# Three row blocks of the first Wq issued from ScalarE's queue behind a GpSimd memset

## The chip, the cores and the metric

The kernel runs on one core of one Trainium2 chip. The metric is the device time of one launch in microseconds (us), from the first instruction to the last. The kernel before takes 1230.46 us (median of three runs, 1230.24 to 1230.65).

## What is computed

The reference is a stack of two equal layers on 2048 tokens of 1024 features in bf16. Each layer is a sliding, dilated attention block (32 heads, window of 8 tokens at distance 2) followed by a dense block:

```
x = A_x
repeat twice:
    x = x + attention(layernorm(x), wqkv, wo)
    x = x + (gelu(layernorm(x) @ w1 + b1) @ w2 + b2)
```

Only the very first step matters here: the layer norm of the first tokens of x, and their product with Wq, which is the first third of the columns of wqkv (1024 rows, 3072 columns).

## The kernel before

The tokens go through the kernel in groups of 512, so there are four groups in each of the two layers, and a group is made of four x tiles of 128 tokens. TensorE (PE) does the matmuls one group and one stage after the other: query, key and value projections, attention output, first and second dense matmul. The other engines work beside it: VectorE (DVE) does the layer norms and the attention products, ScalarE (ACT) moves results out of PSUM and applies functions, GpSimd (POOL) does small operations and some transfers, and SyncE (SP) issues the loads.

**How order is set.** The kernel is written in a tile framework that puts in the semaphore waits. The wrapper `InOrder` around an engine adds order-only edges: while its `on` flag is set, each instruction recorded on this engine comes behind the one recorded before it; otherwise the framework's scheduler may move an instruction. PE's instructions are always chained in the written order. The framework gives every transfer issued by SP or ACT one of eight completion semaphores in turn (called lanes here, 0 to 7), and makes a transfer wait for the earlier transfer on its lane to land before it is issued. The first eight transfers wait for nothing.

**The start.** Before any stage, the kernel issues loads from SP: x tiles 0 and 1, then the first Wq in four pieces with x tiles 2 and 3 between them (`load_wq_piece`, lines 134 to 142). A piece is two row blocks of 128 rows by 1024 columns, 512 KB. `k` numbers the eight row blocks, and a matmul of contraction block `k` needs row block `k` only. A dummy Sqrt (line 151) makes ACT load its table early. `warm_up(14)` gives PE 14 matmuls on zeros while it waits for x.

Then `ln_first` (line 224) normalises the first two x tiles by hand: DVE takes the statistics of tile 0 and tile 1 (`bn_stats`, `bn_aggr`), ACT takes the square roots (`std`, line 238), DVE takes reciprocals and writes the normalised tiles `xn`, PE transposes them, and ACT and DVE copy the transposes out of PSUM into `xnT`. Inside `ln_first` both DVE and ACT are in written order. `build_constants` follows it and fills a mask with GpSimd memsets.

After that `gen_qkv(0)` begins: PE goes over the contraction blocks in four quarters of two `k` each, and within a quarter over seven of eight output chunks, on the 256 tokens of the first two tiles. So the first quarter needs row blocks 0 and 1 of Wq, the second 2 and 3, and so on. Tiles 2 and 3 are transposed on PE in the third and the fourth quarter.

## Time and profile before

| | PE | DVE | ACT | POOL |
|---|---|---|---|---|
| busy us in the span of 1228.4 us | 1221.6 | 861.5 | 315.6 | 120.9 |
| share of the span | 99% | 70% | 26% | 10% |

PE is busy all the time but for the first microseconds. "Busy" on PE also counts the 14 warm-up matmuls, which do no useful work. Over the whole span the loads move 226.64 MB, at 185 GB/s in the mean, with the first two slices of the span (some 61 us) at 302 and 290 GB/s. For this change one has to look at the first 15 us alone: what PE waits for there, and when each transfer is issued and lands. In the listings below SPq is SP's queue of transfers; a "landing" is the time from a transfer's issue to its completion.

### The profile page before, as it was taken

How to read it: one execution, taken by the hardware profiler on the slowest of the kernel's cores; microseconds unless marked ns; L12 is line 12 of the kernel's file. 1: busy time of each engine (PE TensorE's matmuls, PEld its weight loads, DVE VectorE, ACT ScalarE, POOL GpSimd, SP SyncE). 2: the span in 40 equal slices, each digit the busy share in tenths (PEclk: the TensorE clock that was granted, in tenths of full speed). 3: DMA queues.
4: the chain of work that ended last, by engine and by line, in shares of the span. 5: the costliest groups of instructions: out<-in, count | busy, mean ns of one | idle time of the engine just before them, and what ended most of it. 6: DMA issues, size and time to landing. Idle time of an engine off the chain costs nothing.

```text
span 1228.4 us, 13955 instructions
## 1 busy us (share of the span) xinstructions
PE 1221.6 (99%) x5720; PEld 632.7 (52%) x5770; DVE 861.5 (70%) x912; ACT 315.6 (26%) x497; POOL 120.9 (10%) x219
## 2 busy tenths in 40 slices
PE   9999999999999999999999999999999999999998
PEld 7666544456444564446544465444654444444444
DVE  7999896998898999375993759937599797011001
ACT  5343253014310233202431024410244001300310
POOL 2330025010101101100001000000000002000000
PEclk9999999999999999999999999999999999999999
DMA  9965674766638645856557565576664558446441
GB/s 302 290 206 164 176 233 151 202 178 199 219 128 245 188 150 166 239 170 175 161 158 230 172 171 181 157 216 201 171 200 147 186 194 209 149 159 194 156 135 52
DMA packets 223647, 226.64 MB, mean 185 GB/s; under 512 B 71824, under 2 KB 190752, under 8 KB 221536
## 3 DMA queue, kind: packets, MB, share of 16 engines
q1 hardware_dynamic: 214704, 208.69, 56.3%
q0 software_dynamic: 8880, 17.07, 4.2%
q8 instruction: 45, 0.74, 0.2%
q14 instruction: 18, 0.15, 0.0%
HBM read 189.01 MB, written 4.19 MB: 157 GB/s over the span
## 4 chain that ended last, share of the span: by engine, by line
PE 99%; DVE 0%; issue 0%; DMA 0%
PE acc L117 99%; DMA x<-in_A_x_dram 0%; DVE stats L92 0%; PE acc L211 0%; DVE xn L92 0%; DVE x L92 0%; DVE mv L92 0%; DVE rstd L92 0%
## 5 line engine op out<-in xcount | busy, mean ns | idle before, releaser
L117 PE MATMUL acc<-xnT,wt 128*128 128x512 bf16 (+1 forms) x3392 | 720.3, 375 | 0.1
L117 PEld LDWEIGHTS <-wt 128*128 128x128 bf16 x3392 | 400.8, 120 | 317.4
L117 PE MATMUL acc<-wt,hT 128*128 128x512 bf16 (+1 forms) x1780 | 386.0, 376 | 2.1
L117 PEld LDWEIGHTS <-hT 128*128 128x128 bf16 x1820 | 178.1, 98 | 209.0
L92 DVE TENSOR_TENSOR big<-big 128x1024 bf16<-128x1024 bf16 (+2 forms) x184 | 244.8, 1359 | 2.2
L92 ACT ACTIVATE hT<-acc,b1T 128x512 bf16<-128x512 f32 x224 | 152.1, 687 | 325.9 <-PE acc L117 325.8
L92 DVE TENSOR_TENSOR big<-qT,kT 128x4096 bf16<-128x4096 bf16 x64 | 143.8, 2283 | 36.3 <-ACT kT L92 35.9
L92 DVE TENSOR_TENSOR big<-abc,vT 128x4096 bf16<-128x4096 bf16 x64 | 144.6, 2284 | 11.0 <-DMA abc<-a 7.1
L92 DVE TENSOR_TENSOR tmp<-acc,b2bc 128x512 f32<-128x512 f32 x56 | 38.6, 689 | 159.8 <-PE acc L117 156.7
L92 ACT CAST qT<-acc 128x512 bf16<-128x512 f32 (+1 forms) x72 | 38.0, 543 | 276.8 <-PE acc L117 274.6
L117 PE MATMUL acc<-wt,oT 128*128 128x512 bf16 x440 | 97.6, 379 | 0.4
L92 DVE BATCH_NORM_STATS2 stats<-x 128x6 f32<-128x512 bf16 x116 | 77.4, 681 | 6.0 <-DMA x<-in_A_x_dram 5.0
L117 PEld LDWEIGHTS <-oT 128*128 128x128 bf16 x448 | 43.8, 98 | 53.0 <-issue 0.3
L92 DVE TENSOR_TENSOR x<-acc,big 128x512 bf16<-128x512 f32 (+1 forms) x9 | 5.7, 632 | 90.0 <-PE acc L117 90.0
L92 POOL TENSOR_TENSOR rstd<-mv,eps_t 128x1 f32<-128x1 f32 x54 | 16.7, 308 | 524.2 <-DVE mv L92 524.2
L92 ACT CAST vT<-acc 128x512 bf16<-128x512 f32 x64 | 37.4, 585 | 101.9 <-PE acc L117 101.9
L92 ACT CAST kT<-acc 128x512 bf16<-128x512 f32 x64 | 37.3, 584 | 64.5 <-PE acc L117 64.5
L92 DVE TENSOR_TENSOR x<-acc,x 128x512 bf16<-128x512 f32 x64 | 42.9, 670 | 5.1 <-PE acc L117 4.7
L92 DVE TENSOR_SCALAR xn<-x,mv,rstd 128x1024 bf16<-128x1024 bf16 (+2 forms) x53 | 28.5, 540 | 20.1 <-POOL rstd L92 19.9
L92 DVE TENSOR_TENSOR x<-tmp,x 128x512 bf16<-128x512 f32 x56 | 38.6, 689 | 1.4
L92 POOL DMA_DIRECT2D big<-big x24 | 13.3, 563 | 212.5 <-DVE big L92 212.5
L92 ACT ACT_TABLE_LOAD x17 | 21.8, 1283 | 38.9 <-DVE e L92 30.5
(62 smaller groups left out, 285.4 us busy)
## 6 DMA issues: line engine op xcount, KB each, us to landing
wt<-in_B_w_dram SPq DMA_DIRECT2D x56, 1024.0 KB, 5.6
wt<-in_B_w_dram SPq DMA_DIRECT2D x64, 896.0 KB, 4.8
wt<-in_A_wqkv_dram SPq DMA_DIRECT2D x46, 1024.0 KB, 5.6
wt<-in_A_wo_dram SPq DMA_DIRECT2D x16, 1024.0 KB, 5.0
abc<-a POOLq DMA_DIRECT2D x32, 256.0 KB, 4.6
big<-big POOLq DMA_DIRECT2D x24, 256.0 KB, 3.8
x<-in_A_x_dram SPq DMA_DIRECT2D x16, 256.0 KB, 7.1
out_dram<-x SPq DMA_DIRECT2D x31, 128.0 KB, 1.8
```

What stands on the lines that cost most here:

```text
L92: inst = f(*args, **kwargs)
L117: return pe(nc.tensor.matmul(*args, **kwargs))
```

## The change

The change loads Wq one row block at a time, so that a piece is 256 KB. Row blocks 0, 2, 4, 6 and 7 stay on SP's queue, with x tiles 2 and 3 between them as before. Row blocks 1, 3 and 5 are issued from ACT's queue instead. They are to come behind the first two x tiles, and to do so the first of them waits for a GpSimd memset (the first of the small fills of the mask), which takes the place of a clock. `build_constants` is moved ahead of `ln_first` so that the memset exists. The purpose is that a second queue brings parts of Wq while SP issues the rest.

```
-    def load_wq_piece(wt, k):
-        sp.dma_start(wt[:, k % (KD // 2):k % (KD // 2) + 2, :], wqkv_v[:, k:k + 2, 0:D])
+    def load_wq_piece(k, engine):
+        return engine.dma_start(wq_first[k // (KD // 2)][:, k % (KD // 2), :], wqkv_v[:, k, 0:D])
...
     for k in range(0, KD, 2):
-        load_wq_piece(wq_first[k // (KD // 2)], k)
+        load_wq_piece(k, sp)
         if k < 4:
             load_x(0, 2 + k // 2, 3 + k // 2)
+    load_wq_piece(KD - 1, sp)
...
+    act.on = True
     act.activation(one[:], eps_t[:], ACT.Sqrt)
...
         for w in range(W - 1):
-            pool.memset(first[:, w, 0:HALO - DIL * w], -1e9)
+            filled[w] = pool.memset(first[:, w, 0:HALO - DIL * w], -1e9)
         return first
+
+    def load_wq_on_act():
+        act.on = True
+        for k in range(1, KD - 2, 2):
+            load = load_wq_piece(k, act)
+            if k == 1:
+                tc.add_manual_dep(load.ins, filled[0].ins.name,
+                                  mybir.DependencyInfo(mybir.DependencyClass.Sync, mybir.DependencyReason.DATA),
+                                  reason="behind the first x tiles")
+        act.on = False
...
     warm_up(14)
+    first = build_constants()
+    load_wq_on_act()
     ln_first()
-    first = build_constants()
```

## The prediction

> **What bounds the kernel now.** I read the chain of waits first, cut to the first 60 us. Columns: start, length, what.

> ```profile
> 0.74 2.69 DMA x<-in_A_x_dram
> ...
> 3.46 1.30 DVE stats L92 x2
> ...
> 6.44 0.55 DVE xn L92
> ...
> 7.89 0.51 PE acc L211 x6
> 8.40 4.01 PE acc L117 x36
> ...
> 15.05 44.99 PE acc L117 x246
> ```

> Until 8.40 us the chain goes from x tile 0 over the layer norm to the transposes; from 8.40 on it is PE alone (36 matmuls in 4.01 us, 111 ns each), and the page gives PE 99% of the whole chain. So whatever moves the start of these matmuls moves the end by as much, and no Wq piece ends a PE wait today. Next the same start on ACT and PE, from the timeline (start, length, engine, operation, the idle time before it and who ended it).

> ```profile
> 2.04 0.20 ACT L92 ACTIVATE one<-eps_t 128x1 f32<-128x1 f32 x1
> 5.02 0.29 ACT L92 ACTIVATE std<-mv,eps_t 128x1 f32<-128x1 f32 x1 [2.78 <-DVE mv L92]
> 6.42 0.29 ACT L92 ACTIVATE std<-mv,eps_t 128x1 f32<-128x1 f32 x1 [1.10 <-DVE rstd L92]
> ...
> 6.09 0.15 PEld L117 LDWEIGHTS <-big 128*128 128x128 bf16 x1 [0.28 <-issue]
> 7.04 0.57 PEld L211 LDWEIGHTS <-xn 128*128 128x128 bf16 x10 [0.80 <-DVE xn L92]
> ```

> ACT takes the first square root at 5.02, as soon as DVE has the variance; between 2.24 and 5.02 it has nothing to do. PE's warm-up ends about 7.01, right before the first transposes at 7.04. Last, SP's queue:

> ```profile
> 0.74 0.87 SPq L92 DMA_DIRECT2D x<-in_A_x_dram  x2
> 1.66 0.43 SPq L92 DMA_DIRECT2D wt<-in_A_wqkv_dram  x1
> 2.13 0.47 SPq L92 DMA_DIRECT2D x<-in_A_x_dram  x1
> 2.64 0.43 SPq L92 DMA_DIRECT2D wt<-in_A_wqkv_dram  x1
> 3.11 0.47 SPq L92 DMA_DIRECT2D x<-in_A_x_dram  x1
> 3.62 1.40 SPq L92 DMA_DIRECT2D wt<-in_A_wqkv_dram  x2
> 5.06 3.17 SPq L92 DMA_DIRECT2D x<-in_A_x_dram  x4
> 9.24 1.07 SPq L92 DMA_DIRECT2D wt<-in_A_wqkv_dram  x2
> ```

> Issue plus time to landing (the view of the DMA queues, asked in short windows) gives the landings: x0 3.43, x1 4.3, Wq rows 0-1 7.26, x2 7.9, rows 2-3 9.24, x3 9.93, rows 4-5 11.2, rows 6-7 12.6, x4 13.3. The pair at 9.24 starts exactly when rows 2-3 land. That is the lane rule at work: from the ninth transfer on, each waits in SP's queue for the landing of the one eight before it (the pair's first is the thirteenth, rows 2-3 the fifth), and everything behind it waits too. SP's own waits agree:

> ```profile
> SPq L92 <- DMA wt<-in_A_wqkv_dram: 3.8, 4, 1.0
> SPq L92 <- DMA x<-in_A_x_dram: 1.6, 5, 0.3
> ```

> (in total 3.8 us in four waits on wt, 1.6 us in five on x).

> [...] No ACT transfer is in this trace; the mean busy share of the 16 engines, 90% and more from 6 us on at some 385 GB/s[...]. [...] warm-up matmuls start 0.43 us apart to the last, the 512-column key matmuls run at 1.73 us for eight, 0.216 us each. It shows no long idle time of PE, so the fall is not shown.

> **The change part by part.**

> *Smaller pieces on SP.* SP issues nine transfers in place of eight before x4, one more of about 0.45 us. x4 goes out at about 5.06 as before (the single 0.92 us issue falls away or not), and stays behind the same 3 MB. Hidden: x0 and x1 keep their places, and nobody waits for x4 before 13.3. Cost 0. Moving the memsets ahead: POOL has them done by 1.9 us already. Cost 0.

> *The memset wait.* Over by about 1.65 us, when ACT is still in its table load. Cost 0.

> *The lane waits, which the diff does not show.* I read the built order with its waits. SP's transfers take lanes 0 to 7 for x0, x1, row 0, x2, row 2, x3, row 4, row 6; row 7 takes lane 0 again. On ACT, in order behind the dummy Sqrt: row 1 on lane 2, waiting for row 0 to land; row 3 on lane 4, waiting for row 2; row 5 on lane 6, waiting for row 4; and only then the `std` of tile 0. So the first square root, on the chain at 5.02 us today, stands behind the landing of row 4.

> When does row 4 land? Count blocks of 256 KB in landing order. Today block 1 lands at 3.43, 2 at 4.3, 4 at 7.26, 5 at 7.9, 7 at 9.24, 8 at 9.93, 9 about 10.6. In the new SP order row 0 is block 3: between 4.3 and 7.26, I take 5.8. ACT then issues row 1; packets started 1.0 us after issue for x0, so row 1 joins at 6.8. Row 2, block 5, is by then moved and lands at 7.9 undisturbed. Row 3, issued then, joins at 8.9, too late to delay row 4. Row 4 is block 7 with row 1 ahead of it, so eight blocks: 9.93. The bounds are seven blocks (9.24) and nine (10.6).

> Row 5's issue then costs what SP's cost, 0.43 us (0.33 to 0.92), plus 0.05 for the semaphore: `std` of tile 0 at 10.4 in place of 5.02. Both tiles' variances have long been there by then, so after 0.29 us of `std`, 0.07 us and a reciprocal of 0.11 the normalisation `xn` starts at 10.95 in place of 6.44. From there the steps are as today (transposes, copies, matmuls). **4.5 us later**, by the bounds 3.8 to 5.7. The Wq blocks do not bind any more: matmuls start at 12.9, row 3 has landed at about 11.6, and row 5 (issued 10.0, like row 1 about 3.7 us to landing) at 13.7, needed about 3.1 us after 12.9.

> *PE's clock.* Warm-up still ends at 7.01, but the transposes begin at 11.5: 4.5 us idle[...]. If the clock falls, the 16 transposes take 1.7 us in place of 1.35, about 0.4 more, and until about 6 us after 11.5 (warm-up in this trace was slow for 6 us) the matmuls run at half rate: (6.0 - 1.75) / 2 = 2.1 us lost. Sum 2.5[...]; I take 2.4, bounds 0 and 2.5.

> *Later loads.* The scheduler also put the second half of the first Wv behind the DMA transposes of the next groups and behind x13. Today it is issued at 27.0 and PE would need it at 38.1 (the last kT copy starts at 37.21 when the value matmuls begin; the fifth of them, 0.22 us each, is the first to read it). Walking SP's new order with today's transposes (1.3 us each on an idle queue, up to 4.3 beside a load), it is issued between 35 and 41.7 and lands 5.6 us later, 40.7 to 47.3, middle about 43.2; the need moves to 42.6 without and 45 with the clock's fall. I count 0, and up to 2 us on the high side.

> Sum: 4.5 + 2.4 = 6.9 us, so 1237.3.

> **The rivals.** *Blocked, but the clock stays up*: 4.5 us, **1235.0**. [...] *Blocked, but Wq comes faster in small pieces*: the slow stretch between 4.3 and 7.26 goes, each block takes 0.68 us as later, row 4 lands at 4.3 + 5 x 0.68 = 7.7, `xn` at 8.7, 2.3 us[...]: **1232.7**. Against: nothing in the trace ties the slow stretch to the size of a piece; the next piece of two rows took 0.67 us a block. *Wv late*: stall of about 2 us more, **1239.5**. *The second queue works as meant*: ACT's lane waits prove over before it gets to them, rows come in parallel, PE starts at 8.40 as now or a trifle sooner: **1230.2**, not slower. Against: row 4 can't have landed by 5.02, with 1.8 MB ahead of its end and 0.9 MB moved by 5.25.

> **How the numbers follow.** Blocked and clock down 52%; blocked, clock up 30%; small pieces faster 8%; Wv late 6%; as meant 4%. The predicted time is the first. The range leaves out the last three, 18%: from 1234.2 (blocked with the lower bound, 3.8) to 1238.7 (5.7 + 2.5 = 8.2). 0.2% is 2.5 us. Slower: the first, second and fourth case and half of the third, with what the landings leave open, 93%. Same: the rest of the third and half of the last, 5%. Faster 2%.

> **What would show it.** In the changed profile ACT must show three transfers ending about 10 us, `std` right behind them, idle on DVE before the first reciprocal ended by ACT, and PE idle from 7.0 to 11.5 ended by DVE `xn`. The clock shows in the spacing of the first 256-column matmuls, 0.11 or 0.21 us. If `std` stays at 5.02, the argument is wrong as a whole; if it comes at 8, the landings; if PE waits for wt at about 43 us, the Wv case is real.

## The result, and the profile after

The changed kernel takes 1235.38 us (median of five runs, 1234.83 to 1236.43) against 1230.25 us (1230.08 to 1230.65): a ratio of 1.0042, with a 95% interval of 1.0028 to 1.0056. It is 5.1 us slower, and the profiled run (the fastest of the five) has a span of 1233.0 us against 1228.4, 4.6 us longer.

The chain of waits of the changed kernel, cut to the first 70 us (start, length, what):

```profile
...
3.55 5.56 DMA wt<-in_A_wqkv_dram
9.12 0.02 issue
9.14 0.33 ACTq L92
9.47 0.05 issue
9.52 0.30 ACT std L92
9.82 0.02 issue
9.85 0.17 DVE rstd L92
10.02 0.03 issue
10.04 0.56 DVE xn L92
10.60 0.05 issue
10.65 1.89 PE acc L225 x16
12.54 4.44 PE acc L117 x36
...
19.63 50.40 PE acc L117 x271
```

In the kernel before, this chain ran from x tile 0 over VectorE's statistics. Now it runs from a Wq row, through an issue on ScalarE's queue (ACTq), to the first square root. The transfer issued at 3.55 is row 4. It lands at 9.11; row 5, the third transfer on ScalarE, is issued at 9.14, and `std` follows at 9.52 in place of 5.02. The last line starts at 19.63 in place of 15.05, 4.58 us later, and this is the whole difference of the spans (4.6): the rest of the kernel takes as long as before. From 14 us to the end the list of waits has no entry for PE in either kernel.

The timeline of ScalarE and its queue in the changed kernel shows the same from the queue's side:

```profile
2.03 0.20 ACT L92 ACTIVATE one<-eps_t 128x1 f32<-128x1 f32 x1
...
5.97 3.50 ACTq L92 DMA_DIRECT2D wt<-in_A_wqkv_dram  x3
9.52 0.48 ACT L92 ACTIVATE std<-mv,eps_t 128x1 f32<-128x1 f32 x2 [7.28 <-DMA wt<-in_A_wqkv_dram]
```

The three transfers take 3.5 us to issue, because each waits for a landing: rows 0, 2 and 4 land at 1.66 + 4.2 = 5.9, 2.60 + 4.7 = 7.3 and 9.11. The memset was over at 1.6. Behind them ScalarE has sat idle for 7.28 us before `std`, and the view gives a DMA as what ended it, although the variance that `std` needs was there at 5.0.

PE and the clock, in the table of stretches (PE, PEld, DVE, ACT and POOL busy us with instructions, then the granted clock, the DMA share and GB/s):

```profile
9.50:10.00 0.50, 0.00 (x0) 0.00 (x0) 0.15 (x1) 0.48 (x2) 0.00 (x0) 1.00 1.09 418
10.00:10.50 0.50, 0.00 (x0) 0.00 (x0) 0.46 (x2) 0.00 (x0) 0.00 (x0) 0.51 1.04 393
...
13.00:13.50 0.50, 0.50 (x4) 0.40 (x3) 0.47 (x2) 0.50 (x1) 0.00 (x0) 0.58 1.04 381
13.50:14.00 0.50, 0.50 (x7) 0.50 (x6) 0.50 (x2) 0.24 (x1) 0.00 (x0) 1.00 1.19 377
```

PE has nothing to do from 6.94 to 10.65. The clock column goes from 1.00 to 0.51 at 10.0 and comes back to 1.00 at 13.4. (It is of use only from its first change on: it reads 1.00 during the warm-up too, whose 512-column matmuls start 0.43 us apart, where 512-column matmuls later take 0.22 us, 95 of them 20.67 us from 23.63 on in the kernel before.) The mean clock of all five runs lies between 0.997 and 0.999, so the fall isn't special to the profiled one. The same transposes in the kernel before, as the timeline of PE shows them:

```profile
7.05 1.35 PE L211 MATMUL acc<-ident,xn 128*128 128x128 bf16 x16
```

So the 4.58 us have two parts: `xn` of tile 0 starts at 10.04 in place of 6.44, **3.60 us** later; at this half clock (0.50 to 0.51) the 16 transposes take 1.89 - 1.35 = 0.54 us more, and the 36 first matmuls 4.44 - 4.01 = 0.43 us more, together **0.97 us**.

### The profile page after: what moved, and what is told of

Read it like the earlier page. It is cut to its first block, busy times and chain, and to the rows that moved or that the text cites. A ratio compares the mean times of both kernels' runs of the same rounds, so it can differ in the third digit from the quotient of the medians.

```text
span 1233.0 us, 13959 instructions
## 1 busy us (share of the span) xinstructions
PE 1222.4 (99%) x5720; PEld 633.8 (51%) x5770; DVE 861.8 (70%) x912; ACT 315.7 (26%) x497; POOL 124.1 (10%) x219
## 4 chain that ended last, share of the span: by engine, by line
PE 99%; DMA 0%; issue 0%; SPq 0%; DVE 0%; ACTq 0%; ACT 0%
PE acc L117 98%; DMA wt<-in_A_wqkv_dram 0%; PE acc L225 0%; SPq L92 0%; DVE xn L92 0%; DVE x L92 0%; ACTq L92 0%; ACT std L92 0%; DVE rstd L92 0%
## 5 line engine op out<-in xcount | busy, mean ns | idle before, releaser
L117 PE MATMUL acc<-xnT,wt 128*128 128x512 bf16 (+1 forms) x3392 | 720.8, 375 | 0.1
L117 PEld LDWEIGHTS <-wt 128*128 128x128 bf16 x3392 | 401.2, 120 | 317.6
L117 PE MATMUL acc<-wt,hT 128*128 128x512 bf16 (+1 forms) x1780 | 386.0, 376 | 2.1
L117 PEld LDWEIGHTS <-hT 128*128 128x128 bf16 x1820 | 178.1, 98 | 209.0
L92 DVE TENSOR_TENSOR big<-big 128x1024 bf16<-128x1024 bf16 (+2 forms) x184 | 244.8, 1359 | 2.2
L92 ACT ACTIVATE hT<-acc,b1T 128x512 bf16<-128x512 f32 x224 | 152.2, 688 | 325.7 <-PE acc L117 325.5
L92 DVE TENSOR_TENSOR big<-qT,kT 128x4096 bf16<-128x4096 bf16 x64 | 144.1, 2286 | 38.9 <-ACT kT L92 38.5
L92 DVE TENSOR_TENSOR big<-abc,vT 128x4096 bf16<-128x4096 bf16 x64 | 144.6, 2283 | 11.4 <-DMA abc<-a 7.5
L92 DVE TENSOR_TENSOR tmp<-acc,b2bc 128x512 f32<-128x512 f32 x56 | 38.6, 689 | 159.6 <-PE acc L117 156.5
L92 ACT CAST qT<-acc 128x512 bf16<-128x512 f32 (+1 forms) x72 | 38.0, 543 | 276.8 <-PE acc L117 276.7
L117 PE MATMUL acc<-wt,oT 128*128 128x512 bf16 x440 | 97.4, 379 | 0.4
L92 DVE BATCH_NORM_STATS2 stats<-x 128x6 f32<-128x512 bf16 x116 | 77.3, 680 | 3.6 <-DMA x<-in_A_x_dram 2.6
L117 PEld LDWEIGHTS <-oT 128*128 128x128 bf16 x448 | 43.8, 98 | 52.8
L92 POOL TENSOR_TENSOR rstd<-mv,eps_t 128x1 f32<-128x1 f32 x54 | 16.7, 310 | 525.2 <-DVE mv L92 525.2
L92 DVE TENSOR_TENSOR x<-acc,big 128x512 bf16<-128x512 f32 (+1 forms) x9 | 5.7, 632 | 90.0 <-PE acc L117 90.0
L92 ACT CAST vT<-acc 128x512 bf16<-128x512 f32 x64 | 37.5, 586 | 101.7 <-PE acc L117 101.7
L92 ACT CAST kT<-acc 128x512 bf16<-128x512 f32 x64 | 37.3, 585 | 64.5 <-PE acc L117 64.5
L92 DVE TENSOR_TENSOR x<-acc,x 128x512 bf16<-128x512 f32 x64 | 42.9, 671 | 4.6 <-PE acc L117 4.2
L92 DVE TENSOR_SCALAR xn<-x,mv,rstd 128x1024 bf16<-128x1024 bf16 (+2 forms) x53 | 28.6, 541 | 20.2 <-POOL rstd L92 19.9
L92 DVE TENSOR_TENSOR x<-tmp,x 128x512 bf16<-128x512 f32 x56 | 38.6, 689 | 1.4
L92 POOL DMA_DIRECT2D big<-big x24 | 13.3, 564 | 212.5 <-DVE big L92 212.5
```

The source lines that it names most:

```text
L92: inst = f(*args, **kwargs)
L117: return pe(nc.tensor.matmul(*args, **kwargs))
```

## Experiments

The theory: each of ScalarE's three transfers waits for an earlier landing, the first square root stands behind them in the same queue, and PE's clock falls in the idle time that follows. The rivals are: the second queue itself costs time (rows that come through it land late, or slow the x tiles); the smaller pieces do; the clock plays no part.

### The memset wait taken out

```
         for k in range(1, KD - 2, 2):
             load = load_wq_piece(k, act)
-            if k == 1:
-                tc.add_manual_dep(load.ins, filled[0].ins.name, ...)
```

> The changed kernel without the wait for the memset. The built order then gives the three rows on ScalarE lanes that nothing has used, so they wait for no landing (x3 and rows 4, 6, 7 on SyncE wait instead, for x0, x1 and two Wq rows). Lane theory (the time is lost because the first square root stands behind the landing of row 4): rows issued from 2.2 to 3.6 us, std at 5.0, first Wq matmul near 8.3, time 1230.3 (1229.9 to 1231.5, if a late row stalls PE a little). Rival, the second queue itself (rows that come through ScalarE's queue land late, or slow the x tiles): PE still waits for wt or x, time 1233 or more.

Measured: 1230.77 us against 1230.5, ratio 1.0002 (0.9994 to 1.001). Three transfers still go through ScalarE's queue, and the 5 us are gone. The second queue thus has no cost of that size by itself. The first transfer is issued at 0.91, earlier than expected: it doesn't wait for the table load (0.74 to 2.02) or the dummy Sqrt in front of it to finish. It overtakes x1, whose statistics start at 5.38 in place of 4.90; `xn` starts 0.53 us late. That is the harm that the memset wait was meant to prevent.

### A memset one earlier

```
-        pool.memset(first[:], 0.0)
+        filled[-1] = pool.memset(first[:], 0.0)
...
-                tc.add_manual_dep(load.ins, filled[0].ins.name,
+                tc.add_manual_dep(load.ins, filled[-1].ins.name,
```

> The changed kernel with one edit: the first row on ScalarE waits for the memset just before the one it waited for (the fill of z as a whole, done at 1.2 us in place of 1.6). The order then gives the three ScalarE rows lanes that nothing has used. Issue at about 1.25 us, right behind x1, so that x1 keeps its place. Lane theory: no landing is waited for, std at 5.0, PE's first transposes near 7.05 to 7.2, time 1230.2 to 1230.7, that is the whole loss of 5 us goes by a wait that is 0.4 us shorter. Rival, the second queue costs time of its own as soon as x1 is not held up: 1232 or more. No theory expects it below 1229.9, as PE waits for the layer norm and not for Wq.

Measured: 1230.58 us against 1230.47, ratio 1.0001 (0.9993 to 1.0009). ScalarE's queue in this kernel:

```profile
1.26 0.86 ACTq L92 DMA_DIRECT2D wt<-in_A_wqkv_dram  x2
2.04 0.20 ACT L92 ACTIVATE one<-eps_t 128x1 f32<-128x1 f32 x1
2.15 0.45 ACTq L92 DMA_DIRECT2D wt<-in_A_wqkv_dram  x1
5.13 0.29 ACT L92 ACTIVATE std<-mv,eps_t 128x1 f32<-128x1 f32 x1 [2.89 <-DVE mv L92]
```

The rows go out one behind the other, and `std` is at 5.13, ended by VectorE as in the kernel before. The built order tells why. In the changed kernel the three rows stand on lanes 2, 4 and 6 as second users and wait for SyncE's rows 0, 2 and 4; in this one they are the first users of the same lanes, and x3 and rows 4, 6 and 7 on SyncE wait instead, where nothing of the chain is queued behind them. The memset that is waited for ends only about 0.4 us earlier. So the 5 us were not lost by the time of the memset, but by the rows' place in the scheduler's order, and with it their lanes.

### The wait without the second queue

```
+    for k in (1, 3, 5):
+        load_wq_piece(k, sp)
...
     def load_wq_on_act():
         act.on = True
-        for k in range(1, KD - 2, 2):
-            load = load_wq_piece(k, act)
-            ...
+        seen = const.tile([P, 1], F32, name="seen")
+        act.copy(seen[:], wq_first[1][:, 0, 0:1])
```

> All rows on SyncE in the order 0, 2, 4, 6, 7, 1, 3, 5, no transfer on ScalarE; in their place ScalarE copies one element per partition of row 4, in front of the first square root. So the wait for the landing of row 4 is kept and the second queue is gone. Lane theory: row 4 lands at about 9.1, std at about 9.3, PE idle from 7 to about 10.4 and at half clock after it, time as of the changed kernel, 1235.4 less 0.2 (no issue of 0.33 us) , 1234.5 to 1236. Rival, the second queue itself: 1230.3, as nothing goes through it. Rival, later order (row 5 comes last, lands about 11.5, needed at 15): no effect either way.

Measured: 1235.24 us against 1230.5, ratio 1.0039 (1.0026 to 1.0051), the time of the changed kernel with no transfer on ScalarE at all. Its ScalarE lines:

```profile
8.59 0.19 ACT L92 CAST seen<-wt 128x1 f32<-128x1 bf16 x1 [6.35 <-DMA wt<-in_A_wqkv_dram]
8.69 0.48 ACT L92 ACTIVATE std<-mv,eps_t 128x1 f32<-128x1 f32 x2
```

A wait for row 4 in front of the square root is enough. In the profiled run `xn` starts at 9.21, only 2.77 us late, but the half clock (0.50) lasts from 8.4 to 15.2 and costs more: 0.54 us in the transposes and 5.70 - 4.01 = 1.69 us in the 36 matmuls. Sum 5.0 us; the span is 5.1 longer.

### Small pieces alone

```
-    for k in range(0, KD, 2):
+    for k in range(KD):
         load_wq_piece(k, sp)
-        if k < 4:
+        if k in (1, 3):
             load_x(0, 2 + k // 2, 3 + k // 2)
...
-    load_wq_on_act()
```

> One-row pieces, all eight on SyncE in the order 0, 1, x2, 2, 3, x3, 4 to 7; nothing on ScalarE. Takes the size of the pieces by itself. Lane theory: SyncE's ninth transfer on waits for a landing, but no engine of the chain does; std at 5.0, time 1230.3 (within 0.5). Rival, small pieces cost time of their own (slower transfers, a later x3): 1231.5 or more.

Measured: 1230.35 us against 1230.5, ratio 0.9998 (0.999 to 1.0007). The size of the pieces costs nothing that can be measured, and it brings nothing.

### PE kept warm, with and without the second queue

```
-    warm_up(14)
+    warm_up(30)
```

First in the changed kernel:

> The changed kernel with 30 warm-up matmuls in place of 14, so that PE has work until about 10.4 us (6.9 plus 16 at 0.216 us) and its clock need not fall. Clock theory: full clock at the first transposes at 10.65, their 16 in 1.35 us, first Wq matmul chain from 12.0; but rows 1, 3, 5 land at 12.3, 13.6 and 14.9 in the changed kernel, and stall PE by some 0.3 us: time 1234.0 (1233.7 to 1234.6), 1 to 1.4 less than the changed kernel, with a smaller spread than its 1.6 us. If the clock plays no part: 1235.4 as before.

Measured: 1233.93 us against 1230.47, ratio 1.0029 (1.0017 to 1.004); 1.45 us less than the changed kernel. The clock stays at 1.00 in every stretch from 6 to 15 us, and the 16 transposes take 1.35 us. So the clock is part of the loss, and the larger part stays. The 1.45 us are not the clock alone: in the profiled run, the fastest, row 4 landed at 8.24, in the changed kernel's at 9.11, so that the wait was shorter too. Such differences between runs may also be why the spread (1.3 us) is only a little smaller than the changed kernel's 1.6.

Then in the kernel with the wait alone:

> The kernel with the wait alone (all rows on SyncE, ScalarE reads row 4 in front of the first square root) and 30 warm-up matmuls in place of 14. Takes both the second queue and the clock's fall away and leaves the wait. With the landing of row 4 at 8.6 us as in the profile of the wait alone, xn starts at 9.2 in place of 6.44: 2.8 us and nothing else, so 1233.2 (1232.8 to 1233.8) with a spread under 1 us. If the clock's fall were no cost of its own: 1235.2, as with 14. If the late rows were the cause: 1230.5.

Measured: 1233.26 us against 1230.45, ratio 1.0022 (1.0013 to 1.0031), with a spread of 0.8 us. Between the medians the wait by itself thus costs 2.8 us, and the clock's fall 1235.24 - 1233.26 = 2.0 us in the kernel with the wait alone. The profile doesn't show the wait as cleanly. It is of the slowest run: `xn` starts at about 9.05 (`std` at 8.53, and 0.52 us from there as with the wait alone), 2.61 us late, but row 1 lands at 11.26, and the first Wq matmuls start at 11.37, some 0.4 us later than `xn` alone would give. The last line of the start (18.14 in place of 15.05) comes 3.1 us late, of a span that is 3.6 us longer; the rest is lost further back.

### One row on ScalarE

Rows 3 and 5 back on SyncE, row 1 on ScalarE with its memset wait:

```
         load_wq_piece(k, sp)
+        if k + 1 in (3, 5):
+            load_wq_piece(k + 1, sp)
...
-        for k in range(1, KD - 2, 2):
+        for k in (1,):
```

> Only row 1 on ScalarE, with its memset wait; rows 3 and 5 back on SyncE. ScalarE then waits for the landing of row 0 alone, 5.9 us in the changed kernel. Lane theory: issue about 5.9 to 6.3, std of tile 0 at 6.35 in place of 5.02, but xn of tile 0 could not start before 6.44 anyway, so it starts at about 6.85, 0.4 us later; PE idle 0.5 us, no fall of the clock: 1230.7 if row 1 lands by 8.8. But in the changed kernel a row issued on ScalarE took about 6 us to land, which would be 12.3, and then PE waits for row 1 in the first quarter: up to 4 us more, 1234.5. Which of the two it is tells whether late landing through the second queue matters by itself.

Measured: 1236.09 us against 1230.5, ratio 1.004 (1.0027 to 1.0053). One row on ScalarE is no better than three, but the time is lost elsewhere. Its waits (total, times, longest):

```profile
PEld L117 <- DMA wt<-in_A_wqkv_dram: 3.5, 1, 3.5
PE acc L117 <- DMA wt<-in_A_wqkv_dram: 3.4, 1, 3.4
```

`std` comes at 6.16 and the transposes at 7.29, but after one Wq matmul PE stops from about 8.8 to 12.17: row 1, issued at 5.74, lands at 12.13. The clock falls at 10.2, to 0.50, and is back at 17.05. This is a second delay: the row issued on ScalarE's queue behind a busy SyncE landed 6.39 us after its issue. In one of the five runs (1232.81 us) the mean clock was 1.0, so there half clock left no mark and the late landing by itself cost about 2.3 us.

### Why row 1 lands late

In two more kernels row 1 is issued behind `std` of tile 0, on a free lane, so that it blocks nothing. They differ in what SyncE has issued before it, counted in blocks of 256 KB.

```
         stats(0)
+        load_wq_piece(1, act)
-        stats(1)
+        done = stats(1)
+        sp.on = True
+        held = load_wq_piece(2, sp)
+        tc.add_manual_dep(held.ins, done.ins.name, ...)   # only in the second kernel
+        ...   (row 3, x3 and rows 4 to 7 behind it on SyncE)
```

> All rows on SyncE but row 1, which ScalarE issues behind the std of tile 0 at about 5.1 us, on a free lane, so that it blocks nothing. SyncE has issued 9 blocks of 256 KB by then and does not stop. Theory of one line for both queues (a transfer's packets start when the blocks issued before it on the other queue are nearly through): first packet of ScalarE's queue near 8.9 us, row 1 lands at 11 to 12, PE (ready at 8.4) waits about 3 us for it, time 1233 to 1236.5, the clock deciding. Rival, a fixed delay of 3.4 us of that queue: first packet at 8.5, about the same time. Rival, late landing in the one-row kernel came from its wait only: no stall, 1230.4.

> As the kernel with row 1 behind nine blocks, but SyncE holds back row 2 and all behind it until the variance of tile 1 is there (6.4 us), so that only four blocks (x0, x1, row 0, x2) are ahead of row 1 when ScalarE issues it at about 5.1 us. Theory of one line for both queues: first packet of ScalarE's queue at 6 to 6.3 us, row 1 lands by about 7.5, no wait for it; rows 2 to 5 then come later than before and may stall PE by up to 1 us, time 1230.5 to 1231.6. Rival, a fixed delay of 3.4 us: first packet at 8.5, row 1 lands at 10 or later, 1232 or more.

Measured: 1234.55 us (ratio 1.0033, 1.002 to 1.0046) behind nine blocks, 1232.28 us (1.0015, 1.0008 to 1.0022) behind four, both against 1230.47. The DMA issues on ScalarE's queue (count, KB, us from issue to landing), first behind nine blocks:

```profile
wt<-in_A_wqkv_dram ACTq DMA_DIRECT2D x1, 256.0 KB, 6.3
```

and behind four:

```profile
wt<-in_A_wqkv_dram ACTq DMA_DIRECT2D x1, 256.0 KB, 2.7
```

The same transfer takes 6.3 us in the first kernel and 2.7 us in the second. ScalarE's queue (q10 in the list of DMA queues; SyncE's is q1) moves its first packet between 8.5 and 9.0 us in the first, 3.3 us or more after the issue at 5.19, and between 6.4 and 6.5 in the second, about 1 us after the issue at 5.46. A fixed delay of that queue is ruled out. The names of the kernels need a word: in the first, SyncE had in fact issued a tenth block (row 6) at 5.14, and seven of the ten had not landed yet; in the second the data of all four had been moved by about 5.7, so row 1 found the DMA engines idle, and landed as fast as x0 does at the start (2.7 us).

The two kernels also differ in what SyncE issues behind row 1, so a further rival is that SyncE's queue simply goes first. The kernel without the memset wait speaks against it. There row 1 was issued on ScalarE at 0.91, ahead of x1 on SyncE at 1.20. Between 3.0 and 3.5 us the queues moved (packets, MB, share of the DMA engines' time):

```profile
q10 hardware_dynamic: 71, 0.15, 101.1%
q1 hardware_dynamic: 13, 0.01, 6.2%
```

Here SyncE's x1 stands behind ScalarE's row, and lands at 5.36 in place of 4.3. So in these runs it is about the order of issue that counts, across both queues. Which part of the chip keeps that order isn't shown. The order isn't strict: in the kernel behind nine blocks ScalarE's queue had moved one packet by 9.0 us, when SyncE's had moved 2.30 MB of the 2.62 MB (ten blocks) issued ahead of row 1, and from 9.5 to 10.0 us ScalarE's moved 52 packets beside 57 of SyncE's.

In the second kernel the time is lost at rows 4 and 5, which now come late (PE waits 0.93 and 0.36 us for them), so its 1232.28 us lie above the range that was expected. Row 1 landed at 8.2, a little later than the 7.5 expected, but well before the 10 or later of the rival with a fixed delay.

## Why the prediction was right

**The path.** It held that everything hangs on the start of the first Wq matmuls: the span grew by what their chain moved, 4.6 us.

**The lane waits.** The order read from the built program is what the chip did. Rows 1, 3 and 5 are issued as rows 0, 2 and 4 land, and `std` follows. The wait alone gives the same loss, and a wait on another memset, which in effect only moves the lanes, gives none.

**The size of the wait: mis-sized.** Predicted were 4.5 us (3.8 to 5.7), measured 3.60, just under the range of this term. The step that failed is "packets started 1.0 us after issue for x0, so row 1 joins at 6.8". In the profile after, ScalarE's queue moves nothing before 9.3 us, more than 3.3 us after the issue at 5.97, so row 1 stood behind what SyncE had issued and didn't slow row 4, which landed at 9.11 and not at 9.93. The predicted landings of rows 1, 3 and 5 (5.8 + 3.7 = 9.5, 11.6 and 13.7) were low by the same step: row 1 landed at 5.97 + 6.3 = 12.3, the last at 9.14 + 5.8 = 14.9.

**"The Wq blocks do not bind any more": true by a hair.** Row 1 landed at 12.3, and PE's first matmuls started at 12.37. That it didn't bind was luck: the prediction had row 1 landing at 9.5, some 3 us before the matmuls, and not 0.1 us. The two delays of the change lie side by side; with most of the first taken away, as in the one-row kernel, the second comes to light and costs as much.

**The clock: mis-sized.** It fell, as in the prediction's first case, after 3.1 us of idle time (6.94 to 10.0). That it would fall was the author's estimate: the trace of the kernel before has no fall. The predicted cost was 2.4 us; measured are 0.97 in the profiled run, inside the bounds of 0 and 2.5, and 2.0 between the medians of the kernels with the wait alone. The step "until about 6 us after 11.5" took the length of the slow warm-up (0.43 us a matmul) for that of the slow stretch. In the runs the half clock lasted 3.4 us here (10.0 to 13.4) and with nine blocks ahead (11.4 to 14.8), but 6.8 us, twice that, with the wait alone (8.4 to 15.2) and with one row (10.2 to 17.05), and part of it passes while PE is idle anyway (here 0.65 us, 10.0 to 10.65). Which of the two lengths a run gets was not foreseen, and what sets them isn't shown.

**The Wv order.** No cost: PE waits for nothing after 14 us in the changed kernel, where the second half of Wv was issued at 33.3, before the 35 to 41.7 of the prediction.

**The rivals, and luck in the number.** The measured 1235.38 is closest to the rival "blocked, but the clock stays up" (1235.0), not to the predicted 1237.3. The trace shows that this rival is wrong all the same: the clock did fall, and with more warm-up matmuls the time goes down. Its number came near because the wait was 0.9 us shorter than both cases had it, which happens to be about what the clock cost. The prediction's range held because it reached down to that rival. Its sum of 6.9 us was 1.8 over the median's 5.1: 0.9 from the wait and 1.0 to 1.4 from the clock. "As meant" fell with the built order; a kernel that does work as meant exists (the memset one earlier) and takes 1230.58, as that rival said, no better than before. "Faster in small pieces" had row 4 landing at 7.7; it landed between 8.24 and 9.11 in the profiled runs that wait for it, and `xn` was never less than 2.6 us late, where this rival had 2.3. Whether small pieces land a little sooner stays open.

None of these kernels beats the one before. At the start PE waits for the layer norm of the first two tiles, and none of the orders of the Wq rows tried here brings that forward.

## What to carry to other kernels

The transfers put on ScalarE's queue brought their waits along, those too that the framework adds for the reuse of its semaphores, and `std` behind them came at 9.52 in place of 5.02. In a change of this kind, read in the built order what each waits for and what is queued behind it, since a small edit to one dependency can turn the order of the lanes around (a wait on another memset took the 5 us away). Before moving loads to a second queue, ask in the chain of waits whether anything waits for them: here nothing did, so there was nothing to win. And look for the second delay under the first: the row on ScalarE's queue landed 6.3 us after its issue, and hid behind the wait only by chance.
